# FNet mixing plus an MLP on one core: layer norm of blocks 2 and 3 a block sooner, five staging places for the weight forms, and steps behind bank copies

## The chip, the core and the metric

The kernel runs on one core of one Trainium2 chip, as one program and one launch. The metric is the device time in microseconds (us). TensorE is written PE, VectorE DVE, ScalarE ACT, GpSimd POOL and SyncE SP, as the profile writes them. Each engine takes its instructions strictly in the order in which the program issues them, so a step that waits holds everything behind it on the same engine; SP's and ACT's DMA issues stand in those orders too.

## The reference

```python
x = A_x                                   # (1, 2048, 640), float32
xn = layernorm(x, axis=-1)                # eps 1e-5
a = einsum("bsd,ed->bse", xn, dft_hid_re) # hidden DFT, 640 x 640
b = einsum("bsd,ed->bse", xn, dft_hid_im)
y = einsum("ts,bse->bte", dft_seq_re, a) - einsum("ts,bse->bte", dft_seq_im, b)  # 2048 x 2048
h = gelu_tanh(einsum("bsd,df->bsf", xn, w1) + b1)    # 640 -> 1536
out = x + y + (einsum("bsf,fd->bsd", h, w2) + b2)    # 1536 -> 640
```

## The kernel before

**Numbers.** Every product is made of three matmuls: each operand is split into a high and a low part (`split`, lines 160 and 161: ACT copies the high part, DVE subtracts it to get the low part), and high x high, high x low and low x high are added up in a PSUM bank (`product`, lines 277 to 279). A matmul has a 128x128 weight and 512 columns.

**Tokens** are handled in four blocks t = 0 to 3 of 512, that is 16 chunks c of 128 rows; block t has chunks 4t to 4t+3. For one chunk the layer norm is `load_x` (SP), `ln_stats` (DVE), `ln_scale` for four chunks at once (with a square root on ACT), `ln_apply` (DVE, then four stores by SP into the scratch tensor `xs`, line 203). `load_z` (line 234) reads a whole block back from `xs` in another layout, and `transpose_z`, `turn_z2`, `turn_z1` turn it on DVE.

**Stage 1, the MLP of blocks 0 and 1.** The loop over g has 12 steps i for each block; a step is `hidden` (15 matmuls), `gelu` (ACT line 314 and 318, DVE line 320) and `output` (15 matmuls), with the GELU two steps ahead of `output`. Beside block 0's steps runs `first_block(i)`, beside block 1's `second_block(i)`. These hold the layer norm of later blocks, the splits of weights, and from `w_early` the first six steps of `prep_w`.

**`prep_w(s)`** makes the forms of the hidden DFT matrices that the end of the kernel reads back: for column group j = s // 3 it turns two raw pieces (`turn_w`, DVE), and `put_w` splits them by parts into a staging place and stores each into `wits` (line 400). Of the three sub-steps k = s % 3 the first puts two forms, the second two, the third three. During block 1 the staging place is one of two tiles `wst`; later it is one of two halves of the tile `HS`. The store is issued by ACT. A new put into a place waits for the store that last read it.

**Stage 2, the hidden layer of blocks 2 and 3** together, in six passes q, each over two of the twelve units, by a scheme of sums and differences with fewer products. Its inputs (`form_of`: a11, a12, a22, s1 to s4, oa, ob) are made from blocks 2 and 3 (`load_z(2)`, `load_z(3)`) at the end of block 1; its weight sums by `load_rq`, `sums_w1`, `split_w1`. A pass is `head(q)` (12 matmuls), `mid(q)` (21) and `finish(q)` (21). `head` and `mid` hold `copy_bank` (ACT, line 801), which copies a half-finished sum to another bank before PE adds more to the first. `mid` calls `between`, and `outs(1)` (the call `rest`) runs inside `mid(0)`. `act` is the GELU of a pass (line 845). The steps 6 to 14 of `prep_w` run beside passes 1 to 4 (`late_steps`).

**Stage 3, the second layer of blocks 2 and 3**: 24 steps n of 15 matmuls (`second`), with `beside_second(n)`: `split_h` makes the moving operand of two later steps, `late_w2` splits w2, `formed` and `build` make the forms of the rows for stage 4 from pairs of rows `xr` (`load_xr`, line 565) and store the first four, `outs(2)` adds the biased result of block 2 to its x (`load_xo(2)`, line 339) on POOL (line 349), and `load_a` loads the first pieces of the sequence matrices.

**Stage 4** is the sequence DFT and the hidden DFT up to the end, from some 418 us on.

A tile of a pool, or a `place(tag)`, that is opened where another was, waits for all readers and writers of the earlier one. The places `xc01`, `as` and `r01` are used several times in this way; `zo` is one tile shared in turn by z, xo and wz.

Of the kernel before, what the change touches and what calls it, by code (L numbers as in the profile page):

```python
# [26 lines left out]
def kernel(  # L27
# [152 lines left out]
    def ln_stats(c):  # L180
        m = MV
        st = ST[c % 2]
        half = D // 2
        for h in range(2):
            nc.vector.bn_stats(st[:, h, :], xt[c][:, h * half : (h + 1) * half])
        nc.vector.bn_aggr(m[:, c % 4, 0:2], st.rearrange("p a b -> p (a b)"))
# [198 lines left out]
    def put_w(w, j, main, odd=None, negative=False):  # L385

        n = GWIDE[w] * P
        if A["w"]:
            t = A["w"].tile([P, 2, 3 * P], F32R, tag="wst", bufs=2, name=f"wst{w}_{j}")
        else:  # L390
            A["nst"] = A.get("nst", 0) + 1
            t = HS[:, 1 + A["nst"] % 2, :, : 3 * P]
        split(t[:, 0, : 2 * P], t[:, 1, : 2 * P], main)
        if odd is not None and not negative:
            split(t[:, 0, 2 * P :], t[:, 1, 2 * P :], odd)
        elif odd is not None:
            h, l = t[:, 0, 2 * P :], t[:, 1, 2 * P :]
            nc.scalar.activation(h, odd, AF.Copy, scale=-1.0)
            nc.vector.scalar_tensor_tensor(l, odd, -1.0, h.bitcast(F32), op0=ALU.mult, op1=ALU.subtract)
        stores.append(lambda: nc.scalar.dma_start(wits[w][j], t[:, :, :n].bitcast(F32)))  # L400
        if len(stores) == 2:
            put_away()

# [148 lines left out]
    def load_xr(k):  # L552
        if k >= len(builds):
            return
        h, c = builds[k]
        xr[k] = []
        if k == len(builds) - 1:
            A["xcp", 2] = place("xc23", (P, 2, 2, 7 * P))
        for half in range(2):
            if k == len(builds) - 1:  # L560

                r = A["xcp", 2][:, 1, half, :D].bitcast(F32)
            else:
                r = row_tile(f"xr{k}_{half}")
            nc.sync.dma_start(r, xs[half * NS // 2 + h * NK + c])
            xr[k].append(r)
# [171 lines left out]
    def two(lo):  # L738
        return A["zs"][:, lo * TB : (lo + 2) * TB].rearrange("p (a b) -> p a b", a=2)
# [137 lines left out]
    def first_block(i):  # L877

        if i < 2:
            ln_apply(2 * i)  # L880
            ln_apply(2 * i + 1)
            load_x(4 + 2 * i)
            load_x(5 + 2 * i)
        if 2 <= i < 6:
            ln_stats(4 + i - 2)
        if i == 6:
            ln_scale(4, 4)
            for c in range(4, 8):
                ln_apply(c)
            load_z(1)  # L890
            for c in range(8, 12):
                load_x(c)
        if i in (8, 9):
            transpose_z(1, i - 8)
        if 8 <= i < 12:
            ln_stats(i)

    def open_w():
        es_e.close()
# [19 lines left out]
    def second_block(i):  # L919

        if i == 0:
            open_w()
            ln_scale(8, 4)
            for c in range(8, 12):
                ln_apply(c)
            for c in range(12, 16):
                load_x(c)
        if i == 1:
            load_z(2)
        if 2 <= i < 6:  # L930
            ln_stats(10 + i)
        if i == 3:
            A["zs"] = place("xc01", (P, 30 * P), F32, name="zs")
            turn_z2(two(0), 0)
            turn_z2(two(2), 2)
        if i == 4:
            turn_z1(ZT[:, 0], 4)
            form_of("a11", 0, two(0)[:, 0], lane("as", 5))
        if i == 6:
            ln_scale(12, 4)  # L940
            for c in range(12, 16):
                ln_apply(c)
            load_z(3)
            form_of("a11", 1, two(0)[:, 1], lane("xc23", 0))
            form_of("oa", 0, ZT[:, 0], lane("xc23", 1))
            form_of("a12", 0, two(2)[:, 0], lane("xc23", 2))
        if i == 7:
            open_tw()
            open_xf()
        if i == 8:  # L950
            turn_z2(ZT, 2)
            turn_z2(two(4), 0)
            turn_z1(A["zs"][:, 6 * TB : 7 * TB], 4)
            sums_w1(0)
        if i == 9:
            load_xo(1)
            split_w1(0)
            load_rq(1)
            form_of("a22", 0, ZT[:, 0], lane("r01", 0))
            form_of("a22", 1, ZT[:, 1], lane("r01", 1))  # L960
            add(ZT, ZT, two(4))
            form_of("s1", 0, ZT[:, 0], lane("r01", 2))
            form_of("s1", 1, ZT[:, 1], lane("r01", 3))
# [13 lines left out]
        form_of("s4", 0, two(2)[:, 0], XTT[:, 3])  # L977
        form_of("s4", 1, two(2)[:, 1], XTT[:, 4])

    w_early = {1: (0,), 2: (1,), 3: (2,), 4: (3,), 5: (4, 5)}  # L980
    gelu(0, acc0)
    gelu(1, acc1)
    for g in range(NG):
        t, i = divmod(g, NF)
        if t == 0:
# [2 lines left out]
            load_w1(i + 6)  # L988
            load_w2(i + 4)
            first_block(i)  # L990
            if i == 10:
                load_xo(0)
            if i == NF - 1:
                acc = hidden(g + 2)
                output(g)
# [77 lines left out]
    head(1)  # L1073
    finish(0)
    open_wz()
    late_steps = {1: (6, 7), 2: (8, 9), 3: (10, 11), 4: (12, 13, 14)}
    for q in range(1, NF // 2):
        p = q - 1
        if not p % 2:
            act(p, 0, 0)  # L1080
        sums_w1(q + 1)
        act(p, 0, 1)

        def between():
            split_w1(q + 1)
            act(p, 1, 0)
            act(p, 1, 1)

        mid(q, between)
        for k in late_steps.get(q, ()):  # L1090
            prep_w(k)
        load_rq(q + 2)
        if q < NF // 2 - 1:
            head(q + 1)
        else:
            split_h(0)
            second(2, 0, 0, HU[0, 0])
            split_h(1)
            for u in (2, 3, 4):
                split_w2(u)  # L1100
                raw_w2(u + 4, u - 2)
        finish(q)
        if q == 4:
            for u in range(2, 6):
                raw_w2(u, u - 2)

# [8 lines left out]
    A["asb"] = place("as", (P, 48 * P), name="asb")  # L1115
    A["sums"] = A["asb"][:, 20 * P : 38 * P].bitcast(F32).rearrange("p (a b) -> p a b", a=2)

    def formed(k):
        build(k)
        nc.sync.dma_start(forms_ab[k], A["xab", k].bitcast(F32))  # L1120
        nc.sync.dma_start(forms_c[k], A["xc", k].bitcast(F32))

    def late_w2(u):
        split_w2(u)
        if u + 4 < 11:
            raw_w2(u + 4, (u + 2) % 4)

    def beside_second(n):

        if n % 2 and 2 <= (n + 3) // 2 < NF:  # L1130
            split_h((n + 3) // 2)
        if 1 <= n <= 6:
            late_w2(n + 4)
        if n in (2, 4, 6, 8):
            formed(n // 2 - 1)
            load_xr((2, 3, 4, 6)[n // 2 - 1])
# [1 line left out]
            load_xo(2)  # L1138
        if n == 9:
            build(4, "ab")  # L1140
        if n == 10:
            build(6, "ab")
        if n == 11:
            outs(2, (3, 4, 0, 1, 2))
            A["es"].close()
            A["raw"] = pool("rawp")
            load_a(0)
            load_a(1)
        if n == 14:
            A["xcp", 0] = place("xc01", (P, 2, 2, 7 * P))  # L1150
            build(4, "c")
            load_xr(5)
        if n == 16:
            build(5)
        if n == 17:
# [550 lines left out]
```

## Time and profile before

| | |
|---|---|
| time, median of 2 runs | 938.42 us (937.73 to 939.11) |
| profiled execution, own time | 940.44 us |
| its span, first to last instruction | 938.7 us |
| mean granted clock of PE | 0.966 of full speed |
| busy share of the span | PE 92%, DVE 70%, ACT 38%, POOL 2% |
| matmuls | 3711 |
| moved by DMA | 158.43 MB, 169 GB/s in the mean |

How to read it: a busy PE says little about when matmuls are late, so the prediction counts matmuls by stretches of time. In a row of a table of stretches stand the stretch, its length, the busy time of each engine with the number of its instructions in brackets, the granted clock of PE, the busy share of the DMA engines and GB/s. In a timeline row stand the start, the duration, the engine (SPq and ACTq are the issuing of DMAs), the line, the operation, the tiles, the count, and in square brackets the idle time before it with what ended it. In a list of waits stand who waited at which line for whom, the sum in us, the number of times and the longest.

### The profile page before, as it was taken

To read this page: it belongs to the slowest core of one execution; us is meant where nothing else is said; L and a number is where in the kernel's file an instruction comes from. 1 tells how busy PE (TensorE), PEld (TensorE's weight loads), DVE (VectorE), ACT (ScalarE), POOL (GpSimd) and SP (SyncE) were. 2 spreads that over 40 slices of the span, in tenths; PEclk is the share of its full clock that TensorE was granted. 3 is DMA by queue.
4 is the path that set the end of the run, shared out by engine and by line. 5 is a ranking of instruction groups with operands and counts; after the bars stand their busy time and mean duration, and the time that the engine had idled before them with its cause. 6 is when DMAs were issued, how large, how long until landed. Compare 5 with 4: busy or idle time off the path is not lost.

```text
span 938.7 us, 10279 instructions
## 1 busy us (share of the span) xinstructions
PE 866.1 (92%) x3711; PEld 707.4 (75%) x3711; DVE 660.8 (70%) x831; ACT 354.4 (38%) x495; POOL 22.0 (2%) x22
## 2 busy tenths in 40 slices
PE   8999998749765997899999999999999999999997
PEld 6888886537554786677888888888888888888886
DVE  7556535376433395469798888889896889887587
ACT  6444422434332554144334334433232332323241
POOL 0000200003000001100000000000000000000000
PEclk9999999978987899989999999999999999999999
DMA  6746584545553497859487535985475588934355
GB/s 186 221 134 172 113 239 135 128 99 117 155 160 118 138 356 220 202 109 190 103 198 161 148 78 151 319 228 114 130 192 158 181 257 206 291 116 163 97 154 113
DMA packets 214913, 158.43 MB, mean 169 GB/s; under 512 B 82896, under 2 KB 189648, under 8 KB 214352
## 3 DMA queue, kind: packets, MB, share of 16 engines
q1 hardware_dynamic: 201088, 145.08, 59.0%
q10 hardware_dynamic: 13776, 12.72, 3.9%
q8 instruction: 29, 0.48, 0.2%
q14 instruction: 20, 0.16, 0.1%
HBM read 114.76 MB, written 42.99 MB: 168 GB/s over the span
## 4 chain that ended last, share of the span: by engine, by line
PE 58%; DMA 8%; DVE 4%; ACT 2%; SPq 2%; issue 1%; POOL 1%; POOLq 0%; ACTq 0%; DVEq 0%
PE banks L278 19%; PE banks L277 19%; PE banks L279 19%; DMA wit<-hs 3%; DMA forms_c<-xcst 2%; DMA xo<-in_A_x_dram 1%; DMA xr<-xs 1%; SPq L477 1%; DVE hs L161 1%; POOL xo L349 1%; DMA rq<-in_B_w_dram 1%; DVE asb L437 0%; DVE rq L437 0%; ACT xcst L589 0%; DVE rt L497 0%
## 5 line engine op out<-in xcount | busy, mean ns | idle before, releaser
L278 PE MATMUL banks<-as,xab 128*128 128x512 f32 x411 | 160.2, 390 | 0.8 <-DVE as L161 0.8
L279 PE MATMUL banks<-as,xab 128*128 128x512 f32 x411 | 160.2, 390 | 0.0
L277 PE MATMUL banks<-as,xab 128*128 128x512 f32 x411 | 160.1, 390 | 0.0
L160 ACT ACTIVATE as<-r 128x1024 fp32r<-128x1024 f32 x80 | 85.0, 1062 | 175.0 <-PE banks L279 148.5
L161 DVE TENSOR_TENSOR as<-r,as 128x1024 fp32r<-128x1024 f32 x80 | 97.2, 1216 | 38.5 <-ACT as L160 38.4
L278 PEld LDWEIGHTS banks<-as,xab 128*128 128x128 f32 x411 | 77.3, 188 | 17.4 <-DVE as L161 1.2
L279 PEld LDWEIGHTS banks<-as,xab 128*128 128x128 f32 x411 | 77.3, 188 | 16.1
L277 PEld LDWEIGHTS banks<-as,xab 128*128 128x128 f32 x411 | 77.3, 188 | 16.0
L277 PE MATMUL banks<-as,xc 128*128 128x512 f32 x224 | 87.1, 389 | 0.0
L278 PE MATMUL banks<-as,xc 128*128 128x512 f32 x224 | 87.1, 389 | 0.0
L279 PE MATMUL banks<-as,xc 128*128 128x512 f32 x224 | 87.1, 389 | 0.0
L160 ACT ACTIVATE as<-rt 128x1024 fp32r<-128x1024 f32 x32 | 34.0, 1062 | 69.9 <-PE banks L279 57.9
L301 PE MATMUL banks<-xtt,xab 128*128 128x512 f32 x240 | 56.7, 390 | 0.0
L301 PEld LDWEIGHTS banks<-xtt,xab 128*128 128x128 f32 x240 | 44.9, 188 | 9.5 <-DVE xtt L161 0.2
L278 PEld LDWEIGHTS banks<-as,xc 128*128 128x128 f32 x224 | 42.0, 188 | 8.8
L279 PEld LDWEIGHTS banks<-as,xc 128*128 128x128 f32 x224 | 42.0, 188 | 8.8
L277 PEld LDWEIGHTS banks<-as,xc 128*128 128x128 f32 x224 | 42.0, 188 | 8.7
L320 DVE TENSOR_TENSOR hs<-ab,hs 128x512 fp32r<-128x512 f32 x24 | 17.6, 735 | 40.2 <-ACT hs L318 40.1
L161 DVE TENSOR_TENSOR as<-rt,as 128x1024 fp32r<-128x1024 f32 x32 | 38.8, 1212 | 5.3 <-ACT as L160 5.3
L497 DVE STREAM_TRANSPOSE r<-raw 128x1024 f32<-128x1024 f32 x32 | 39.5, 1240 | 1.5 <-PE banks L279 1.0
L160 ACT ACTIVATE as<-u 128x1024 fp32r<-128x1024 f32 (+1 forms) x24 | 22.1, 919 | 48.2 <-PE banks L279 48.2
L437 DVE TENSOR_TENSOR r<-r,rt 128x1024 f32<-128x1024 f32 x32 | 38.9, 1219 | 0.1
(328 smaller groups left out, 1625.7 us busy)
## 6 DMA issues: line engine op xcount, KB each, us to landing
raw<-in_A_dft_seq_re_dram SPq DMA_DIRECT2D x64, 256.0 KB, 5.2
raw<-in_A_dft_seq_im_dram SPq DMA_DIRECT2D x64, 256.0 KB, 5.3
ws<-wit SPq DMA_DIRECT2D x15, 384.0 KB, 5.7
x<-in_A_x_dram SPq DMA_DIRECT2D x16, 320.0 KB, 4.4
xs<-x SPq DMA_DIRECT2D x64, 80.0 KB, 1.8
xo<-in_A_x_dram SPq DMA_DIRECT2D x16, 320.0 KB, 6.7
xab<-wit SPq DMA_DIRECT2D x13, 384.0 KB, 4.0
wit<-hs ACTq DMA_DIRECT2D x12, 384.0 KB, 3.8
```

The source lines that it names most:

```text
L160: nc.scalar.activation(h, s, AF.Copy)
L161: nc.vector.tensor_tensor(l, s, h.bitcast(F32), op=ALU.subtract)
L277: nc.tensor.matmul(acc, wh, mh, start=first, stop=False, skip_group_check=goes_on)
L278: nc.tensor.matmul(acc, wh, ml, start=False, stop=False, skip_group_check=goes_on)
L279: nc.tensor.matmul(acc, wl, mh, start=False, stop=last, skip_group_check=goes_on)
L301: nc.tensor.matmul(acc, W1[i][:, a, j * P : (j + 1) * P], XT[j][:, b], start=n == 0, stop=n == len(steps) - 1)
L320: nc.vector.tensor_tensor(hs[:, 1], a, hs[:, 0].bitcast(F32), op=ALU.subtract)
L349: eng.tensor_tensor(d, d, yt.rearrange("p (n i) -> p n i", i=B), op=ALU.add)
L437: nc.vector.tensor_tensor(dst, a, b, op=op)
L477: nc.sync.dma_start(raw[g][q * B : (q + 1) * B], v[:, :, s0 : s0 + NK * B])
L497: nc.vector.transpose(held(pieces[g][2], u).rearrange("p c (n i) -> p c n i", i=B), r.rearrange("p n (c i) -> p c n i", i=B))
```

## The change

- **Layer norm.** In `first_block` the statistics of chunks 8 to 11 move from steps 8 to 11 into steps 8 and 9; the scaling, the stores of block 2's rows and the loads of chunks 12 to 15 move from step 0 of `second_block` to step 10 of `first_block`. In `second_block`, `load_z(2)` moves from step 1 to 0, the statistics of chunks 12 to 15 from steps 2 to 5 into 0 and 1, their scaling and stores from step 6 to 2, `load_z(3)` from 6 to 3, `turn_z1` of z2 from 4 to 3, the opening of the pool `xf` with `load_rq(0)` from 7 to 5, the turns of z3 with `sums_w1(0)` from 8 to 7, `load_xo(1)` from 9 to 7, `split_w1(0)` and `load_rq(1)` from 9 to 8. Step 5 of `prep_w` moves from step 5 to step 6.
- **Staging.** From step 6 of `prep_w` on, a put goes to one of five places in a new tile at `xc01` instead of two in `HS`, and SP issues the store instead of ACT.
- **Order in a pass.** `prep_w` comes behind `head(q + 1)` instead of ahead of it; `load_rq(q + 2)` moves into `between`; step 14 moves behind `finish(4)`; the split of w2 unit 4 moves from pass 5 to step 1 of stage 3.
- **Stage 3.** The rows of build 5 are loaded at the start, into a free part of the place `as`, instead of at step 14; the first two parts of build 6 move from step 10 to 12, behind `outs(2)`; `load_a(1)` moves from 11 to 13.

```diff
--- before.py
+++ after.py
@@ -388,8 +388,8 @@
         if A["w"]:
             t = A["w"].tile([P, 2, 3 * P], F32R, tag="wst", bufs=2, name=f"wst{w}_{j}")
         else:
-            A["nst"] = A.get("nst", 0) + 1
-            t = HS[:, 1 + A["nst"] % 2, :, : 3 * P]
+            A["nst"] = A.get("nst", -1) + 1
+            t = A["wst"][:, A["nst"] % 5 * 6 * P :][:, : 6 * P].rearrange("p (a b) -> p a b", a=2)
         split(t[:, 0, : 2 * P], t[:, 1, : 2 * P], main)
         if odd is not None and not negative:
             split(t[:, 0, 2 * P :], t[:, 1, 2 * P :], odd)
@@ -397,7 +397,7 @@
             h, l = t[:, 0, 2 * P :], t[:, 1, 2 * P :]
             nc.scalar.activation(h, odd, AF.Copy, scale=-1.0)
             nc.vector.scalar_tensor_tensor(l, odd, -1.0, h.bitcast(F32), op0=ALU.mult, op1=ALU.subtract)
-        stores.append(lambda: nc.scalar.dma_start(wits[w][j], t[:, :, :n].bitcast(F32)))
+        stores.append(lambda: (nc.scalar if A["w"] else nc.sync).dma_start(wits[w][j], t[:, :, :n].bitcast(F32)))
         if len(stores) == 2:
             put_away()
 
@@ -560,6 +560,8 @@
             if k == len(builds) - 1:
 
                 r = A["xcp", 2][:, 1, half, :D].bitcast(F32)
+            elif k == 5:
+                r = A["asb"][:, (38 + 5 * half) * P : (43 + 5 * half) * P].bitcast(F32)
             else:
                 r = row_tile(f"xr{k}_{half}")
             nc.sync.dma_start(r, xs[half * NS // 2 + h * NK + c])
@@ -892,8 +894,15 @@
                 load_x(c)
         if i in (8, 9):
             transpose_z(1, i - 8)
-        if 8 <= i < 12:
-            ln_stats(i)
+            ln_stats(2 * i - 8)
+            ln_stats(2 * i - 7)
+        if i == 10:
+            load_xo(0)
+            ln_scale(8, 4)
+            for c in range(8, 12):
+                ln_apply(c)
+            for c in range(12, 16):
+                load_x(c)
 
     def open_w():
         es_e.close()
@@ -920,42 +929,41 @@
 
         if i == 0:
             open_w()
-            ln_scale(8, 4)
-            for c in range(8, 12):
+            load_z(2)
+            ln_stats(12)
+            ln_stats(13)
+        if i == 1:
+            ln_stats(14)
+            ln_stats(15)
+        if i == 2:
+            ln_scale(12, 4)
+            for c in range(12, 16):
                 ln_apply(c)
-            for c in range(12, 16):
-                load_x(c)
-        if i == 1:
-            load_z(2)
-        if 2 <= i < 6:
-            ln_stats(10 + i)
         if i == 3:
             A["zs"] = place("xc01", (P, 30 * P), F32, name="zs")
             turn_z2(two(0), 0)
             turn_z2(two(2), 2)
+            turn_z1(ZT[:, 0], 4)
+            load_z(3)
         if i == 4:
-            turn_z1(ZT[:, 0], 4)
             form_of("a11", 0, two(0)[:, 0], lane("as", 5))
+        if i == 5:
+            open_xf()
         if i == 6:
-            ln_scale(12, 4)
-            for c in range(12, 16):
-                ln_apply(c)
-            load_z(3)
             form_of("a11", 1, two(0)[:, 1], lane("xc23", 0))
             form_of("oa", 0, ZT[:, 0], lane("xc23", 1))
             form_of("a12", 0, two(2)[:, 0], lane("xc23", 2))
         if i == 7:
             open_tw()
-            open_xf()
-        if i == 8:
             turn_z2(ZT, 2)
             turn_z2(two(4), 0)
             turn_z1(A["zs"][:, 6 * TB : 7 * TB], 4)
+            load_xo(1)
             sums_w1(0)
-        if i == 9:
-            load_xo(1)
+        if i == 8:
             split_w1(0)
             load_rq(1)
+        if i == 9:
             form_of("a22", 0, ZT[:, 0], lane("r01", 0))
             form_of("a22", 1, ZT[:, 1], lane("r01", 1))
             add(ZT, ZT, two(4))
@@ -977,7 +985,7 @@
         form_of("s4", 0, two(2)[:, 0], XTT[:, 3])
         form_of("s4", 1, two(2)[:, 1], XTT[:, 4])
 
-    w_early = {1: (0,), 2: (1,), 3: (2,), 4: (3,), 5: (4, 5)}
+    w_early = {1: (0,), 2: (1,), 3: (2,), 4: (3,), 5: (4,), 6: (5,)}
     gelu(0, acc0)
     gelu(1, acc1)
     for g in range(NG):
@@ -988,8 +996,6 @@
             load_w1(i + 6)
             load_w2(i + 4)
             first_block(i)
-            if i == 10:
-                load_xo(0)
             if i == NF - 1:
                 acc = hidden(g + 2)
                 output(g)
@@ -1073,7 +1079,8 @@
     head(1)
     finish(0)
     open_wz()
-    late_steps = {1: (6, 7), 2: (8, 9), 3: (10, 11), 4: (12, 13, 14)}
+    A["wst"] = place("xc01", (P, 30 * P), name="wstp")
+    late_steps = {1: (6, 7), 2: (8, 9), 3: (10, 11), 4: (12, 13)}
     for q in range(1, NF // 2):
         p = q - 1
         if not p % 2:
@@ -1083,24 +1090,25 @@
 
         def between():
             split_w1(q + 1)
+            load_rq(q + 2)
             act(p, 1, 0)
             act(p, 1, 1)
 
         mid(q, between)
-        for k in late_steps.get(q, ()):
-            prep_w(k)
-        load_rq(q + 2)
         if q < NF // 2 - 1:
             head(q + 1)
         else:
             split_h(0)
             second(2, 0, 0, HU[0, 0])
             split_h(1)
-            for u in (2, 3, 4):
+            for u in (2, 3):
                 split_w2(u)
                 raw_w2(u + 4, u - 2)
+        for k in late_steps.get(q, ()):
+            prep_w(k)
         finish(q)
         if q == 4:
+            prep_w(14)
             for u in range(2, 6):
                 raw_w2(u, u - 2)
 
@@ -1115,6 +1123,8 @@
     A["asb"] = place("as", (P, 48 * P), name="asb")
     A["sums"] = A["asb"][:, 20 * P : 38 * P].bitcast(F32).rearrange("p (a b) -> p a b", a=2)
 
+    load_xr(5)
+
     def formed(k):
         build(k)
         nc.sync.dma_start(forms_ab[k], A["xab", k].bitcast(F32))
@@ -1122,15 +1132,15 @@
 
     def late_w2(u):
         split_w2(u)
-        if u + 4 < 11:
+        if u + 4 < NF - 1:
             raw_w2(u + 4, (u + 2) % 4)
 
     def beside_second(n):
 
         if n % 2 and 2 <= (n + 3) // 2 < NF:
             split_h((n + 3) // 2)
-        if 1 <= n <= 6:
-            late_w2(n + 4)
+        for u in {1: (4, 5), 2: (6,), 3: (7,), 4: (8,), 5: (9,), 6: (10,)}.get(n, ()):
+            late_w2(u)
         if n in (2, 4, 6, 8):
             formed(n // 2 - 1)
             load_xr((2, 3, 4, 6)[n // 2 - 1])
@@ -1138,18 +1148,18 @@
             load_xo(2)
         if n == 9:
             build(4, "ab")
-        if n == 10:
-            build(6, "ab")
         if n == 11:
             outs(2, (3, 4, 0, 1, 2))
             A["es"].close()
             A["raw"] = pool("rawp")
             load_a(0)
+        if n == 12:
+            build(6, "ab")
+        if n == 13:
             load_a(1)
         if n == 14:
             A["xcp", 0] = place("xc01", (P, 2, 2, 7 * P))
             build(4, "c")
-            load_xr(5)
         if n == 16:
             build(5)
         if n == 17:
```

## The prediction

> **What bounds the kernel now.** PE is busy for 92% of the span, so I looked for the stretches in which its matmuls are not back to back. The table of stretches, cut where its gaps begin and end:
>
> ```profile
> 145.00:186.00 41.00, 32.34 (x130) 24.82 (x128) 18.43 (x44) 16.91 (x31) 0.00 (x0) 0.96 0.42 123
> 186.00:205.00 19.00, 5.96 (x19) 4.52 (x20) 13.50 (x17) 5.58 (x10) 0.00 (x0) 0.64 0.71 142
> 205.00:222.00 17.00, 12.88 (x43) 9.72 (x42) 12.91 (x19) 8.54 (x15) 7.27 (x5) 0.80 0.38 92
> 222.00:312.00 90.00, 65.50 (x249) 50.94 (x248) 36.62 (x79) 33.90 (x71) 0.00 (x0) 0.87 0.48 136
> 312.00:364.00 52.00, 50.59 (x222) 41.33 (x221) 35.26 (x66) 26.77 (x48) 0.00 (x0) 1.00 0.80 285
> 364.00:374.00 10.00, 4.84 (x16) 3.54 (x16) 5.97 (x10) 6.43 (x11) 3.15 (x3) 0.83 0.54 100
> 394.00:418.00 24.00, 18.01 (x66) 13.97 (x65) 18.71 (x29) 9.85 (x16) 0.00 (x0) 0.79 0.40 92
> 440.00:915.00 475.00, 475.00 (x2098) 393.21 (x2097) 398.41 (x364) 165.94 (x169) 0.00 (x0) 1.00 0.64 173
> ```
>
> The last row sets the scale: 475 us for 2098 matmuls is 0.2264 us each, clock 1.00. Nothing is to be won there, and what is won earlier passes whole to the end. Length less matmuls x 0.2264 is what each other stretch loses, slow clock included: 11.6, 14.7, 7.3, 33.6, 1.7, 6.4 and 9.1 us, together 84.4. The list of PE's waits names the causes:
>
> ```profile
> PE banks L277 <- ACT banks L801: 24.0, 5, 10.4
> PE banks L277 <- ACT r L160: 14.6, 1, 14.6
> PE banks L277 <- ACT hs L318: 6.5, 2, 4.1
> PE banks L277 <- ACT xtt L160: 5.5, 1, 5.5
> PE banks L277 <- DVE ot L347: 5.2, 1, 5.2
> PE banks L277 <- ACT pb L845: 4.4, 2, 3.2
> ```
>
> These waits make 60.2 us; most of the other 24 is slow clock and half-fed restarts after them. So the question is, for each wait, what made ACT or DVE late, and whether the change takes that away.
>
> **Block 1 (145 to 205, 26.3 lost).**
>
> ```profile
> 92.30 0.88 DVE L185 BATCH_NORM_STATS2 st<-x 128x6 f32<-128x320 f32 x2
> 119.47 0.69 ACT L314 ACTIVATE ab<-banks,b1c 128x512 f32<-128x512 f32 x1 [0.87 <-DVE wt L437]
> 131.57 7.80 SPq L364 DMA_DIRECT2D wraw<-in_A_dft_hid_re_dram  x4
> 165.69 0.69 ACT L314 ACTIVATE ab<-banks,b1c 128x512 f32<-128x512 f32 x1 [1.06 <-DVE wst L161]
> 169.51 2.18 DVE L201 TENSOR_SCALAR x<-x,mv 128x640 f32<-128x640 f32 x4
> 170.15 8.93 SPq L203 DMA_DIRECT2D xs<-x  x16
> 180.66 1.91 SPq L234 DMA_DIRECT2D z<-xs  x4
> 189.00 1.25 DVE L730 STREAM_TRANSPOSE zt<-z 128x1024 f32<-128x1024 f32 x1 [14.15 <-DMA z<-xs]
> 199.02 1.29 DVE L161 TENSOR_TENSOR r<-zt,r 128x512 fp32r<-128x512 f32 x2 [0.69 <-ACT r L160]
> ACT wst L160 <- DMA wit<-wst: 16.8, 7, 5.4
> ```
>
> The GELU of step 6 starts at 165.69, the scaling that follows it ends at 171.7, 16 stores take SP until 179.1, block 3 is read from 180.66 and is there at 189.00, and the form for which PE waits 14.6 us (s1) is done 11.3 us later, at 200.3. After the change the scaling follows step 2, whose GELU starts at 119.47: with the same 6.0 us the rows are ready at 125.5. On SP stand ahead of their stores the loads of the next wraw pieces, after step 1's turn at about 118, at worst twice 7.80 us: 134. Stores to 143, z3 issued then and landed 8.3 us after: 152 at worst, s1 possible at 163. PE, without the 14.6 and without the some 10 us lost before, asks for it at 199.0 - 24.6, about 174. So this wait goes with 11 us in hand.
>
> What is late next is ACT itself. Line 318's 6.5 us come from puts that wait for their stores; in block 1 the places stay two and ACT still issues, so much of the 16.8 us of store waits stays. What lightens it: step 5 moves to a step of its own, and DVE no longer meets rows that have not landed. The GELU runs two steps ahead, two times 30 matmuls, 13.6 us; that cover bore the first lag before. I keep 3 us of loss, with 0 and 10 (all that was lost before the z wait) as ends.
>
> The moved parts in block 0: two more chunks of statistics (0.88 and an aggregate each, some 2.2 us) stand ahead of block 1's operand on DVE in step 9. PE waits for nothing there now; the cover is 30 matmuls of `output`, 6.8 us, so 0; uncovered it would be 2.2. Square roots and their table loads keep their number. SP's 16 stores and four loads move ahead of `outs(0)`'s stores, and wraw and z2 stand behind both; all are awaited steps later. `load_z(2)` has to wait for the landed stores of block 0's output (one tile `zo`), as before. Gain 26.3 - 3 = 23.3.
>
> **The first `copy_bank` (205 to 222, 7.3 lost).**
>
> ```profile
> 204.24 0.58 ACT L808 ACTIVATE fifth<-banks 128x512 f32<-128x512 f32 x1
> 212.45 0.58 ACT L801 ACTIVATE banks<-banks 128x512 f32<-128x512 f32 x1 [1.51 <-DVE ab L347]
> ```
>
> From `fifth` to the end of this copy ACT and DVE need 8.8 us in one chain (forms of s3, weight sums, ob, bias and transposition of one bank), which the change leaves alone. But `fifth` was late, behind forms waiting for z3. Now it can follow its matmuls, and PE has 30 more (6.8 us) before it needs the copy: 2.0 stay, 5.3 go. Ends: 0 and 7.3.
>
> **The passes (222 to 312, 33.6 lost).** Groups of instructions in this stretch, the store's own issue, and the last put before the longest wait:
>
> ```profile
> L161 DVE TENSOR_TENSOR hs<-wz,hs 128x256 fp32r<-128x256 f32 (+1 forms) x30 | 10.5, 378 | 21.9 <-ACT hs L160 21.9
> L160 ACT ACTIVATE hs<-wz 128x256 fp32r<-128x256 f32 (+1 forms) x30 | 10.4, 380 | 32.9 <-DMA wit<-hs 25.3 <-DVE wz L372 5.4 <-DVE wz L437 2.0
> L437 DVE TENSOR_TENSOR rq<-rq 128x256 f32<-128x256 f32 (+1 forms) x12 | 6.2, 513 | 11.9 <-DMA rq<-in_B_w_dram 11.6
> L437 DVE TENSOR_TENSOR banks<-banks,fifth 128x512 f32<-128x512 f32 x9 | 6.1, 694 | 5.1 <-ACT banks L801 4.8 <-PE banks L279 0.3
> L437 DVE TENSOR_TENSOR wz<-wz 128x256 f32<-128x256 f32 (+1 forms) x15 | 5.9, 395 | 0.2
> L161 DVE TENSOR_TENSOR tw<-rq,tw 128x1024 fp32r<-128x1024 f32 x4 | 4.9, 1226 | 11.9 <-ACT tw L160 11.9
> L372 DVE STREAM_TRANSPOSE wz<-wz 128x640 f32<-128x640 f32 x6 | 4.7, 820 | 0.0
> L400 ACTq DMA_DIRECT2D wit<-hs x21: 520/521/592, 233.1 to 304.1; - x21
> 303.23 0.42 ACT L160 ACTIVATE hs<-wz 128x256 fp32r<-128x256 f32 x1 [2.75 <-DMA wit<-hs]
> ```
>
> ACT sat 25.3 us waiting for stores to leave the two halves of HS, and `copy_bank` stood behind it. Three things go. Five places take the puts of a whole pass (4, 5, 5, 4, then 3): a place is used again a pass later, so the 25.3 go. The 21 issues (0.52 each, 10.9 us) leave ACT. And the copies now stand ahead of the steps. `load_rq` ahead of the wz loads on SP takes the 11.6 us of DVE too, which stand behind the 4.4 of line 845.
>
> What remains: ACT's puts over four passes are 10.4 busy + 5.4 + 2.0 = 17.8, 4.5 a pass, and stand between `fifth` and the next copy, where PE has 36 matmuls, 8.2 us. DVE's six rows make 38.3, 9.6 a pass, against 54 matmuls, 12.2 us. So neither binds in the mean; passes 1 and 4, with two turns and the three dependent sums, do more than their quarter, and step 14 adds three puts ahead of the last copy. I keep 1.5 us a pass, 6, with 0 and 16 as ends.
>
> New waits: SP's stores stand ahead of later loads on SP, each until DVE has its low part; behind them wait the w2 loads of units 2 to 5, needed only after pass 5 and a step of stage 3 (21 + 15 + 21 + 15 matmuls, 16 us). The split of w2 unit 2 now waits until the last staging store has left `xc01`, with the same cover. Gain 27.6.
>
> [...]
>
> **Stage 3 (364 to 374 and 394 to 418).**
>
> ```profile
> 361.78 8.83 DMA xo<-in_A_x_dram
> 364.74 0.52 ACT L589 ACTIVATE xab<-xr 128x384 fp32r<-128x384 f32 x1 [5.53 <-DMA xr<-xs]
> 370.85 5.03 POOL xo L349 x4
> 386.83 8.19 DMA xr<-xs
> 395.10 0.52 ACT L589 ACTIVATE xab<-xr 128x384 fp32r<-128x384 f32 x1 [14.10 <-DMA xr<-xs]
> ```
>
> The second place first: PE waits for a `split_h` that stands on ACT behind build 5, which waits 14.1 us for its rows, because they were issued at 386.83. They are now loaded some 60 us sooner, into free columns of `as`; SP waits there for the last weights in `as` (end of pass 5), and behind it stand only loads that wait for stage 3 anyway. 9.1 lost, 0.5 stays: gain 8.6.
>
> The first place I expect to move, not to go. Build 6 (5.53 us for rows) no longer holds up `outs(2)`, so PE gets its two banks in time. But POOL's first add still waits for xo, landed at 370.6 by the chain, and two buffers let DVE turn only two banks before that. The other three come after POOL's adds, 1.26 us each, so at about 375.4; then build 6 and the `split_h` that PE needs after 12 + 30 matmuls, 9.5 us behind 364.5: wanted at 374.0, there at about 379. That is as long a gap as the 5.2 now. Gain 0; ends -1 and 6.4.
>
> **How the numbers follow.** 23.3 + 5.3 + 27.6 + 8.6 = 64.8 us from the profiled execution's own 940.44 gives 875.6; the median shown is 2.0 lower than that execution, so **874**, chance 0.57, own range 864 to 885.
>
> Rivals. **Block 1 stays held** (0.12): ACT's store waits in two places let the GELU come late, all 10 stay instead of 3, and the first copy keeps its 7.3: 886. For it: 16.8 us of waits untouched; against: the x rows no longer stop DVE. **The passes become hand-over bound** (0.10): ACT and DVE take turns 30 times, DVE's idle 21.9 in its row stays in part, 16 us stay instead of 6: 884; with the former together 896. Against: of that idle most is the stores'. **Only the issues leave ACT** (0.04): stores land so much later from SP's fuller queue that places are still waited for, and 10.9 of the 33.6 us go instead of 27.6: 890. Against: the row at 303.23 waited for a place used two puts before; now it is five. **xo does not matter** (0.08): if the first place goes too, 867. **The order stands on paper only** (0.05): wraw, stores and z3 queue on SP so that s1 comes after 174; it would have to be 11 us later than my worst case, and then up to 14.7 return: 888. **Slower than before** (0.04): the clock. If the denser matmuls made the granted clock fall through the 475 us and after, the gain of 65 would be used up where it falls under 0.88 (2098 x 0.2264 / 0.88 = 540). Against: 475 us at 1.00 in this trace. [...]
>
> The range, with the two mishaps together on one side and all ends good on the other: 858 to 898. Two runs of this kernel differ by 0.15%, but about 2% is what a measurement can tell from no change: faster than 919.7 has 0.92, within 2% 0.05, slower 0.03.
>
> **What would show it.** Right: z's landing some 40 us sooner and no wait for line 160's r; no put waiting for a store after 222 and line 801's wait under 4 us in all; no wait of build 5 for xr; a gap near the middle of block 3's second layer, ended by a `split_h` behind DVE's transpositions, with POOL waiting for xo. Wrong: long waits for line 318 still in block 1, a turn of wz waiting for its loads in pass 1, or SP's stores holding back rq.

## The result and the profile after

The changed kernel takes **876.99 us** (876.81 to 877.18) against 938.42 before: ratio 0.9345, 95% interval 0.9305 to 0.9386. Its profiled execution has a span of 875.0 us and an own time of 876.81.

First the table of engines on its page, then the table of stretches, cut again where the gaps begin and end (stretch, length, busy time of each engine with its instructions, granted clock, DMA share, GB/s):

```profile
PE 849.2 (97%) x3711; PEld 698.5 (80%) x3711; DVE 659.7 (75%) x831; ACT 354.0 (40%) x495; POOL 21.2 (2%) x22
```

```profile
145.00:181.00 36.00, 33.45 (x144) 26.50 (x143) 23.60 (x42) 15.63 (x31) 0.00 (x0) 1.00 0.72 189
181.00:200.00 19.00, 13.41 (x47) 10.08 (x46) 14.48 (x22) 9.92 (x18) 7.26 (x5) 0.82 0.38 90
200.00:254.00 54.00, 54.00 (x240) 44.72 (x239) 34.93 (x77) 30.95 (x66) 0.00 (x0) 1.00 0.66 186
254.00:316.00 62.00, 60.20 (x263) 49.02 (x263) 38.41 (x71) 34.76 (x62) 0.99 (x1) 1.00 0.88 300
316.00:331.00 15.00, 9.83 (x32) 7.35 (x32) 13.03 (x24) 5.44 (x10) 5.41 (x5) 0.77 0.74 153
331.00:376.00 45.00, 44.18 (x196) 36.24 (x195) 34.04 (x43) 18.92 (x26) 0.00 (x0) 1.00 0.87 168
376.00:851.00 475.00, 475.00 (x2097) 393.47 (x2096) 398.45 (x364) 165.98 (x169) 0.00 (x0) 1.00 0.64 173
```

The last stretch, the sequence DFT, is what it was: 475 us, 2097 matmuls, clock 1.00. All that changed lies ahead of it, and PE's busy time (849.2) is now 97% of the span. Length less matmuls x 0.2264, against what the prediction left standing:

| part | lost before | forecast to stay | stays |
|---|---|---|---|
| block 1 (145 to 181) | 26.3 | 3 | 3.4 |
| first `copy_bank` (181 to 200) | 7.3 | 2.0 | **8.4** |
| passes (200 to 254), and their hand-over to stage 3 (254 to 316) | 33.6 | 6 | 0 and 2.5 |
| stage 3, first place (316 to 331) | 6.4 | 6.4 | 7.8 |
| stage 3, second place (331 to 376) | 9.1 | 0.5 | 0.6 |

Together 22 to 23 us stay where the prediction left 19.6 (with 1.7 between the passes and the first place). PE's list of waits (who waited where for whom: us, times, longest) has changed as much:

```profile
PE banks L277 <- ACT banks L803: 5.0, 1, 5.0
PE banks L277 <- ACT xtt L160: 3.3, 1, 3.3
...
PE banks L278 <- DVE xtt L161: 1.9, 1, 1.9
...
PE banks L277 <- ACT r L160: 0.8, 1, 0.8
```

Line 803 is `copy_bank` (801 before): 24.0 us in five waits have become one of 5.0. The 14.6 for line 160's r (the form of s1) is down to 0.8. The 3.3 and 1.9 are the `split_h` of stage 3's first place.

### The profile page after: what moved, and what is told of

Same layout as the page of the kernel before. It is cut to its first block, busy times and chain, and to the rows that moved or that the text cites. A ratio compares the mean times of both kernels' runs of the same rounds, so it can differ in the third digit from the quotient of the medians.

```text
span 875.0 us, 10292 instructions
## 1 busy us (share of the span) xinstructions
PE 849.2 (97%) x3711; PEld 698.5 (80%) x3711; DVE 659.7 (75%) x831; ACT 354.0 (40%) x495; POOL 21.2 (2%) x22
## 4 chain that ended last, share of the span: by engine, by line
PE 74%; DMA 7%; DVE 7%; ACT 4%; SPq 3%; issue 2%; POOL 1%; ACTq 0%; DVEq 0%; POOLq 0%
PE banks L278 23%; PE banks L279 23%; PE banks L277 23%; PE banks L301 4%; DMA forms_c<-xcst 2%; DMA wit<-wst 2%; POOL xo L349 1%; DMA x<-in_A_x_dram 1%; DMA xo<-in_A_x_dram 1%; DMA xs<-x 1%; SPq L876 1%; SPq L364 1%; DMA wraw<-in_A_dft_hid_im_dram 1%; SPq L203 1%; DVE xtt L161 0%
## 5 line engine op out<-in xcount | busy, mean ns | idle before, releaser
L161 DVE TENSOR_TENSOR as<-u,as 128x1024 fp32r<-128x1024 f32 (+1 forms) x24 | 24.9, 1042 | 18.8 <-ACT as L160 18.8
```

The lines of the kernel that those rows point to most:

```text
L161: nc.vector.tensor_tensor(l, s, h.bitcast(F32), op=ALU.subtract)
```

## Experiments: one part undone at a time

Each kernel below is the changed one with one part put back. Times stand beside 876.99.

**u_ln: the layer norm and `second_block` as before.**

```diff
-        if i == 10:
-            load_xo(0)
-            ln_scale(8, 4)
...
+        if i == 6:
+            ln_scale(12, 4)
+            for c in range(12, 16):
+                ln_apply(c)
+            load_z(3)
```

> The changed kernel with the layer norm of blocks 2 and 3 and the steps of second_block put back where they were before. If the parts add up, the losses of block 1 (26.3 us before, 3.7 now) come back and the first copy stays near 8: about 22 us more, 899. If the passes ran well only because block 3's data came early, the copies of the passes wait again and it goes over 910. If the layer norm is not the cause of the gain in block 1, it stays under 885.

Measured 900.06 us, ratio 0.9598 (0.9574 to 0.9623): 23.1 more. The wait list of that run:

```profile
PE banks L277 <- ACT r L160: 14.3, 1, 14.3
PE banks L277 <- ACT hs L318: 6.2, 2, 4.1
```

The old waits of block 1 (14.6 and 6.5) are back to within 0.3 us, and the passes still lose nothing. The sooner layer norm, with the steps of `second_block` that moved along with it, therefore pays for block 1 by itself; the two were not run apart.

**u_stage, u_two, u_act: the staging.** The first has two halves of HS and ACT's stores again (the new order stays), the second two halves with SP's stores, the third five places with ACT's stores.

```diff
# u_stage and u_two
-            t = A["wst"][:, A["nst"] % 5 * 6 * P :][:, : 6 * P].rearrange("p (a b) -> p a b", a=2)
+            t = HS[:, 1 + A["nst"] % 2, :, : 3 * P]
# u_stage and u_act
-        stores.append(lambda: (nc.scalar if A["w"] else nc.sync).dma_start(wits[w][j], t[:, :, :n].bitcast(F32)))
+        stores.append(lambda: nc.scalar.dma_start(wits[w][j], t[:, :, :n].bitcast(F32)))
```

> The changed kernel with the old staging (two halves of HS, stores issued by ACT) and the new order in a pass. My theory, that places are the larger part: puts wait some 25 us for stores again, 6.3 us a pass beside the 4.5 of the puts, against 8.2 us of cover, so 2 to 3 us a pass come back: about 10 more, 887. Rival, that the order alone does it, because the copies stand ahead: within 3 us of 877. Rival, that the places alone do it: the whole 33 us come back, 910.

> The changed kernel with SP issuing the stores, but two halves of HS as places. My theory: the waits for stores come back in full, some 20 to 25 us of ACT, and most of the 20 us with them: 890 to 897. Rival, that the issuer counts: under 882.

> The changed kernel with five places, but the stores issued by ACT again. My theory, that the places carry the 20 us which the old staging cost: only 21 issues of some 0.5 us and their waits for DVE's low parts come back to ACT, about 4 us a pass beside 4.5 of puts, within or just over the cover of 8.2: 877 to 881. Rival, that ACT must not issue: half of the 20 us or more come back, 887 or over.

| | two places | five places |
|---|---|---|
| ACT issues | 896.62 (ratio 0.9555, 0.9532 to 0.9578) | 885.17 (0.9436, 0.9415 to 0.9457) |
| SP issues | 893.56 (0.9519, 0.9505 to 0.9533) | 876.99 |

ACT's waits for stores and the stretch of the passes in u_stage, then the same waits in u_two; in the third fence u_act's waits of ACT between 225 and 275 us, and its stores by line:

```profile
ACT hs L160 <- DMA wit<-hs: 19.9, 11, 2.7
...
217.00:284.00 67.00, 52.30 (x192) 39.93 (x191) 32.26 (x64) 29.30 (x58) 0.00 (x0) 0.85 0.52 159
```

```profile
ACT hs L160 <- DMA wit<-hs: 20.2, 9, 5.2
```

```profile
ACT wstp L160 <- DVE wstp L161: 2.6, 2, 1.3
ACT pa L847 <- DVE wstp L161: 2.1, 2, 1.1
L400 ACTq DMA_DIRECT2D wit<-wstp x21: 326/327/632, 211.1 to 258.8; - x21
```

Two places make ACT wait 20 us for stores whoever issues them, so the places are the larger part: 16.6 us with SP as issuer, 11.5 with ACT. The issuer is worth 3.1 us while the places still block (the two intervals touch), and 8.2 once they do not. I had expected at most 4 of it; the u_act expectation is a miss. So is u_stage's: 887 was expected, or 910 if the places did it all, and 896.62 came, 19.6 more. u_two's was right. The last row is the line of the stores: 21 issues of 0.33 to 0.63 us, added up one by one 8.9 us. That alone could make the 8.2. The two rows above it point at a second cost: an issue on ACT comes after DVE's low part, and the next put or GELU (line 847) stands behind it. How the 8.2 divide between the two was not separated.

**u_order: `prep_w` ahead of `head(q + 1)` again**, five places and SP kept.

```diff
         mid(q, between)
+        for k in late_steps.get(q, ()):
+            prep_w(k)
```

> The changed kernel with five places and SP's stores, but with the steps of prep_w ahead of head(q + 1) again. My theory: without store waits a pass's puts are some 4.5 us of ACT, and PE has 27 matmuls (6.1 us) between the copy's source and its use, so 0 to 6 us come back in all: 877 to 883. Rival, that the order is what counts: the copies are late by the puts each pass and 15 to 20 us come back, 892 to 897.

Measured 876.21 us, 0.9342 (0.9321 to 0.9363), the same. With five places the order of the steps is worth nothing: no put waits any more, so it does not matter whether the copy stands behind it. With two places it may well matter (33.6 us lost in the passes before, 23.5 in u_stage, 67.00 - 192 x 0.2264), but the order alone with two places was not run.

**u_xr5: the rows of build 5 at step 14 again.**

```diff
-    load_xr(5)
...
             build(4, "c")
+            load_xr(5)
```

> The changed kernel with the rows of build 5 loaded at step 14 again. My theory: build 5 waits for rows behind SP's loads of the sequence matrices and holds up a split_h: a gap near 345 us of some 9 us, 886. Rival, that the gap near 318 already pays for it, because PE comes later there: under 3 us more, 880.

Measured 886.40 us, 0.9448 (0.9422 to 0.9474): 9.4 more, and ACT's timeline has the old wait back:

```profile
339.18 0.53 ACT L589 ACTIVATE xab<-xr 128x384 fp32r<-128x384 f32 x1 [10.68 <-DMA xr<-xs]
```

## Experiments: what still stands

**e_xo2: `load_xo(2)` at step 7 of stage 3 instead of 8.** In the changed kernel, timelines of SP, POOL, DVE and ACT at the first place:

```profile
301.46 1.85 SPq L567 DMA_DIRECT2D xr<-xs  x2
303.36 2.97 SPq L339 DMA_DIRECT2D xo<-in_A_x_dram  x4
315.01 6.40 POOL L349 TENSOR_TENSOR xo<-xo,ot 128x512 f32<-128x512 f32 x5 [117.20 <-DMA xo<-in_A_x_dram]
316.34 0.72 DVE L347 STREAM_TRANSPOSE ot<-banks 128x512 f32<-128x512 f32 x1 [9.66 <-POOL xo L349]
320.32 0.42 ACT L591 ACTIVATE xab<-asb 128x256 fp32r<-128x256 f32 x1 [10.10 <-DVE asb L437]
322.89 1.21 DVE L161 TENSOR_TENSOR xtt<-pb,xtt 128x1024 fp32r<-128x1024 f32 x1
```

xo is issued at 303.36, behind the stores and row loads of step 8, and is there at 315.01. DVE's third transposition waits 9.66 us for POOL; build 6 (line 591) waits 10.10 behind it; the low part of the `split_h` that PE needs is done at 324.1.

```diff
+        if n == 7:
+            load_xo(2)
...
-        if n == 8:
-            load_xo(2)
```

> The changed kernel with the load of x for block 2 (load_xo(2)) at step 7 of stage 3, ahead of the forms and rows of step 8 on SP, instead of behind them. My theory, that xo's late landing holds DVE's transpositions and behind them build 6 and split_h(8): xo lands some 8 us sooner and the gap near 318 (3.4 + 2.2 us and slow clock, 8.0 in all) goes to 0 to 2, 869 to 871. Rival, that POOL's adds or build 6 set it: the gap stays over 4 us, 874 or more.

Measured **868.94 us** (868.87 to 870.88), ratio 0.9264 (0.925 to 0.9278), and the place as a stretch of its trace, with SP's and POOL's rows:

```profile
316.00:331.00 15.00, 15.00 (x68) 12.43 (x67) 13.09 (x28) 8.36 (x14) 0.00 (x0) 1.00 1.16 230
...
296.18 2.96 SPq L339 DMA_DIRECT2D xo<-in_A_x_dram  x4
...
308.46 6.28 POOL L349 TENSOR_TENSOR xo<-xo,ot 128x512 f32<-128x512 f32 x5 [110.63 <-DMA xo<-in_A_x_dram]
```

PE is busy for all 15 us where it was busy for 9.83. Loading xo 7 us sooner (296.18 against 303.36) removed the whole gap, so its late landing was the cause. This version beats both kernels.

**e_outs0 and e_chain: the first `copy_bank`.** ACT in the changed kernel, from the forms of s2 to the copy:

```profile
180.05 0.63 ACT L160 ACTIVATE xfx<-zt 128x512 fp32r<-128x512 f32 x1 [3.16 <-issue]
181.62 0.58 ACT L810 ACTIVATE fifth<-banks 128x512 f32<-128x512 f32 x1
186.20 1.06 ACT L160 ACTIVATE tw<-rq 128x1024 fp32r<-128x1024 f32 x1 [2.44 <-DVE rq L437]
187.68 0.64 ACT L344 ACTIVATE banks<-banks,b2c 128x512 f32<-128x512 f32 x1
189.84 0.58 ACT L803 ACTIVATE banks<-banks 128x512 f32<-128x512 f32 x1 [1.51 <-DVE ab L347]
```

e_outs0 puts the eviction of `outs(1, (0,))` (line 344) ahead of the weight sums. e_chain, built on e_xo2, puts `sums_w1(1)`, `split_w1(1)`, `load_rq(2)` and the form ob behind the copy, at the head of `rest`.

```diff
# e_outs0
+    outs(1, (0,), yt=lambda n: AB[:, 0], done=False)
     sums_w1(1)
...
# e_chain
     def rest():
+        sums_w1(1)
+        split_w1(1)
+        load_rq(2)
+        form_of("ob", 0, A["zs"][:, 6 * TB : 7 * TB], HS[:, 0])
         outs(1, (2, 1, 3, 4), yt=lambda n: AB[:, (n + 1) % 2])
```

> The changed kernel with outs(1, (0,)), which frees the bank for the first copy, ahead of the sums and the split of the next weights and of ob. My theory, that the first copy is late because these 3.5 us of ACT and DVE stand ahead of it: the gap of 5.2 us near 185 falls under 2 and its slow clock goes, 5 to 8 us less, 869 to 872. Rival, that the forms of s2 and s3, which come late from block 3, set it: 1 us or less, 876.

> Built on the kernel that loads xo of t = 2 at n = 7 (868.94 us). `sums_w1(1)`, `split_w1(1)`, the load of rq and the form ob go behind the first `copy_bank`, so that only the eviction of `outs(1, (0,))` stands ahead of it. Theory A (the copy stands behind that work on ScalarE): the eviction runs at about 183.9, its transposition at 184.6, the copy ends near 186 in place of 190.4 and the wait of 5.0 us ends under 1.5; but the banks of `head(1)` then wait for `outs(1, (2, ...))`, which gives back 2 to 4 of the 6 us: 864 to 867 us. Rival B (VectorE is busy without a break from 177 to 199 and only the place of the stall changes): 868 to 870 us.

e_outs0 takes 877.16 us, 0.9348 (0.9331 to 0.9366). e_chain takes 868.83, 0.9263 (0.925 to 0.9275), beside e_xo2's 868.94. Neither gains, as both rivals said. In e_outs0 the copy itself still stands on ACT behind the split of the weights and starts at 188.79 instead of 189.84, so e_chain is the real test. PE's waits, e_outs0 first, then e_chain:

```profile
PE banks L277 <- ACT banks L803: 4.4, 1, 4.4
```

```profile
PE banks L277 <- DVE ab L347: 3.7, 1, 3.7
...
PE banks L277 <- ACT banks L803: 0.5, 1, 0.5
```

In e_chain the copy is no longer late (0.5 us), but PE then waits 3.7 us for the next bank to be turned by DVE; the place loses 8.2 us in place of 8.6 (both counted from the starts of the matmuls). The stall moved behind the next thing that DVE had to do. So the place of the copy on ACT alone is not what costs; the forms, sums and transpositions from some 177 to 199 us are DVE's and ACT's work, and it starts late.

**e_turn, best2 and e_z3: starting it sooner**, all built on e_xo2. DVE stands idle for 5.60 us ahead of 162.66 in the changed kernel. e_turn moves z3's three transpositions there from step 7 (ahead of `prep_w(5)`), and a22 and s1 from step 9 to 8; best2 is e_turn with e_chain; e_z3 is e_turn with the scaling and stores of rows 12 to 15 at step 1.

```diff
# e_turn, best2, e_z3: in step 6
             form_of("a12", 0, two(2)[:, 0], lane("xc23", 2))
+            turn_z2(ZT, 2)
+            turn_z2(two(4), 0)
+            turn_z1(A["zs"][:, 6 * TB : 7 * TB], 4)
# e_z3 also
             ln_stats(15)
-        if i == 2:
             ln_scale(12, 4)
```

> Built on the kernel that loads xo of t = 2 at n = 7 (868.94 us). The three transpositions of z3 stand at the end of step 6 of block 1 in place of step 7, and the forms a22 and s1 follow at the end of step 8 in place of step 9. Theory A: the loss of 8.6 us around the first `copy_bank` is what VectorE has left to do late: it stands idle for 5.60 us ahead of 162.66 and is then busy from 165 to 185 almost without a break, so that `fifth` and the copy come behind the forms of s2. With the transpositions (3.1 us) in that idle stretch the forms of s2 end some 3 us sooner, the copy too, and 8.6 becomes 5 to 6: 865 to 867 us. Rival B: ScalarE's wait for the stores of the staged forms (6.17 us to 162.22) and the order of the steps on ScalarE hold the forms where they are: 868 to 870 us.

> Both of these edits on the kernel that loads xo of t = 2 at n = 7 (868.94 us). If both theories A hold, the work of VectorE that ends at 199 ends 3 us sooner and the copy no longer waits for it: 8.6 us lost become 2 to 4, 862 to 865 us. If both rivals hold: 868 to 870 us.

> The kernel with the transpositions of z3 at the end of step 6 (877.77 us, 10.0 us lost in one place of block 1), and `ln_scale` and `ln_apply` of rows 12 to 15 at step 1 of block 1 in place of step 2, ahead of `prep_w(0)` and its loads. Theory A (z3 lands too late: its stores stand behind the loads and stores of the forms of wr and wi, so that it is loaded at 156 and lands at 164): the stores go out near 118 to 128, z3 is loaded near 138, right behind the last transposition of z2, the transpositions wait for nothing, the 10 us of block 1 go, and the forms of s1 and s2 end sooner, so that the first copy loses 3 to 6 us in place of 8.6: 862 to 867 us. Rival B (the copy is late by VectorE's and ScalarE's own work from 165 on, z3 or not): the 10 us go, the first copy stays at 8 to 9: 868 to 870 us. Rival C (z3's load does not come sooner, the place of the stores alone moves): 876 to 879 us.

e_turn and best2 fell outside both theories; e_z3 has the time of its rival C, though not by C's mechanism. e_turn takes 877.77 us (0.9352, 0.9339 to 0.9364), best2 877.81 (0.9353, 0.934 to 0.9366) and e_z3 877.33 (0.9352, 0.934 to 0.9365), some 9 us over e_xo2. DVE and ACT in e_turn, and PE's wait:

```profile
164.28 1.25 DVE L732 STREAM_TRANSPOSE zt<-z 128x1024 f32<-128x1024 f32 x1 [8.09 <-DMA z<-xs]
167.58 1.20 ACTq L400 DMA_DIRECT2D wit<-wst  x2
172.06 0.42 ACT L160 ACTIVATE wst<-wt 128x256 fp32r<-128x256 f32 x1 [16.23 <-DMA wit<-wst]
PE banks L277 <- ACT hs L318: 9.9, 1, 9.9
```

z3 is not there before 164.28. The idle stretch was no room to use: the transposition in it waits 8.09 us, DVE's low parts of step 5 wait behind it, so their stores leave at 167.58 instead of 156.67; the third put needs one of the two places, waits 16.23 us on ACT, and the GELU behind it stops PE for 9.9. In e_z3, SP and ACT:

```profile
123.98 18.79 SPq L203 DMA_DIRECT2D xs<-x  x16
143.78 1.98 SPq L364 DMA_DIRECT2D wraw<-in_A_dft_hid_re_dram  x4
148.05 2.47 SPq L234 DMA_DIRECT2D z<-xs  x4
173.27 0.42 ACT L160 ACTIVATE wst<-wt 128x256 fp32r<-128x256 f32 x1 [9.21 <-DMA wit<-wst]
```

z3 is loaded 8 us sooner (148.05, against 156.00), and DVE no longer waits for it. But the 16 stores take SP 18.8 us, the loads of the next weight pieces go out at 143.78 instead of 123.76, and step 5's third put still holds ACT until 173.27. Its GELU stops PE for 6.6 us, and the clock granted in 145 to 181 is 0.91, where the changed kernel has 1.00. So block 1 in the changed kernel is in balance by little: z3's loads, the weight pieces on SP and the two staging places hold each other, and each move sooner made another late. The first copy came no sooner either: it starts at 197.29 in e_turn and at 198.50 in e_z3, against 189.84 in the changed kernel, because everything behind that put came later. Whether block 1 with more staging places would let the first copy go was not run.

## Why the prediction was right, and where its steps were off

874 was forecast, 877 came; the sum against the profiled executions was 64.8 us, and 940.44 - 876.81 = 63.6 were measured. Of the miss 1.2 us are the sum's; the rest is the step from the profiled execution to the median, put at -2.0, where the two agree after the change (876.81 and 876.99). That the sum came so close is in part luck: the first copy kept 6.4 us more than forecast, the passes with their hand-over 5.2 less (2.5 for 6 and 1.7). The low end of the range is not quite its sum: with all four good ends another 17.4 us go from 874, which gives about 857, not 858.

**Block 1: right in size, wrong in its working.** The gain is as forecast (3.4 us stay), and u_ln shows that the layer norm makes it. But z3 was forecast to land by 152 at worst, with 11 us in hand. SP in the changed kernel, with its waits for those stores between 130 and 175 us, then ACT and DVE:

```profile
132.99 2.07 SPq L364 DMA_DIRECT2D wraw<-in_A_dft_hid_im_dram  x4
140.94 13.50 SPq L203 DMA_DIRECT2D xs<-x  x16
156.00 2.12 SPq L234 DMA_DIRECT2D z<-xs  x4
SPq L203 <- DMA wit<-wst: 12.2, 3, 5.8
162.22 0.42 ACT L160 ACTIVATE wst<-wt 128x256 fp32r<-128x256 f32 x1 [6.17 <-DMA wit<-wst]
165.08 0.69 DVE L320 TENSOR_TENSOR hs<-ab,hs 128x512 fp32r<-128x512 f32 x1 [1.99 <-ACT hs L318]
165.69 1.24 DVE L732 STREAM_TRANSPOSE zt<-z 128x1024 f32<-128x1024 f32 x1
176.40 1.29 DVE L161 TENSOR_TENSOR r<-zt,r 128x512 fp32r<-128x512 f32 x2 [0.70 <-ACT r L160]
```

The weight loads were out at 135 (forecast: 134 at worst). Then, by the profile, the stores of x waited 12.2 us for the stores that ACT issues from `wst`, a wait that I did not count; they ended at 154.4 instead of 143, and s1 was ready at 177.7 instead of 163. The whole of the 11 us was used up, and not by z3 alone. The transposition at 165.69 has no idle time ahead of it, so z3 was there by then (in e_turn, which issues it at 155.81, it is there at 164.28). DVE came to it behind the GELU of its step, whose low part starts at 165.08, and that GELU stood on ACT behind the put that waited 6.17 us for a store. The 163 counted the transpositions from z3's landing; they stand in step 7, and DVE came to step 7 only at 165.69.

PE lost only 0.8 us there because its own demand came at about the same time, 176. That is luck: the 11 us in hand were gone. The rival "the order stands on paper only" had its condition met (s1 after 174), but not its price of up to 14.7. The sign "z's landing some 40 us sooner" failed too: the transposition starts 23 us sooner, at 165.69 against 189.00.

**First copy: the step that failed.** "Now it can follow its matmuls" was the step. The chain from `fifth` to the copy took 181.62 to 190.42, 8.8 us as forecast. But `fifth` still stands on ACT behind the forms of s2, which come at 180 to 181, while the last matmul that it needs starts at 178.19. The term of 2.0 measures 8.4 (its upper end was 7.3), and it is the largest miss; line 801's wait, now 803, is 5.0 where under 4 was the sign. An estimate from these rows: with `fifth` at 178.6 the copy would have ended near 187.4, some 2 us after PE ran out of matmuls at about 185.3, as forecast. The other 3 us of the wait of 5.0 are `fifth`'s lateness, and the slow clock after the wait (0.58 granted in 190 to 197), which the term left out, is most of what is left of the 8.4.

e_chain shows that this is no matter of the order on ACT alone. That z3's landing is the cause is not shown: in e_z3 its transpositions start at 164.33 without a wait, and the copy is later still. What ACT and DVE did late in all three kernels (the changed one, e_turn, e_z3) comes behind step 5's third put and its wait for a store, to 162.22, 172.06 and 173.27. Whether that put is the cause stays open; a version that removes the loss was not found.

**Passes: right, and over-kept.** No put waits after 200, `copy_bank`'s waits there are gone, and PE is busy for 54.00 of 54 us: of the 6 kept, 2.5 stay, and those at the hand-over to stage 3. The two-by-two table gives the staging its size, 19.6 us, and the rival that only issues leave ACT fell: five places with ACT as issuer already gain 11.5. What won the rest of the 33.6 no run separates; u_stage differs from the kernel before in the order and in `load_rq`, and in block 1 and stage 3. That rival's 10.9 was the time of the 21 issues themselves in the kernel before (0.52 us each). In the runs the issuer saved 3.1 or 8.2 us by the places beside it, and u_act's issues come to 8.9.

**Stage 3: right.** The second place went (u_xr5 brings it back with 9.4 us, forecast 8.6). The first moved and did not go, by the mechanism told: xo's landing, POOL, DVE's transpositions, build 6, `split_h`. It costs 7.8 instead of 6.4, a little past the term's end of 1 us more, and e_xo2 removes it by moving xo alone. The rival in which xo does not matter (867) is refuted as a reason, though e_xo2 ends near its number.

**Rivals on the clock and on the order.** The granted clock is 1.00 through the 475 us as before, so the denser matmuls cost nothing there. The order of `prep_w` is worth nothing beside five places; the prediction counted it among three causes of one gain, and could not have told them apart.

## What to carry to other kernels

Find for each wait of the bound engine the one resource behind it, and ask what it has to be late for next: here the number of staging places was worth 11 to 17 us, while e_chain's new order on ACT moved a stall without shortening it. An idle stretch on an engine is room only for work whose data are there (in e_turn DVE waited 8.09 us in it); look up the landing of the load, not the start of the idle time, before moving a step into it. The other way round, data that land sooner gain nothing while the step that uses them stands behind a step that waits (in the changed kernel z3's transposition behind the put that waited 6.17 us); look up both times, and take the later one. When moving a load on a shared queue, price all that is queued around it, stores of other engines' staging included (12.2 us of waits for the stores of x).

## What the runs showed of the hardware

**A stall of PE can cost more than its length, and does not always.** PE's rows in u_two, with the stretch around them (clock 0.79), and in u_ln, each after a gap:

```profile
220.32 0.50 PE L277 MATMUL banks<-xtt,tw 128*128 128x512 f32 x1 [1.87 <-ACT banks L803]
...
221.88 0.63 PE L277 MATMUL banks<-as,xab 128*128 128x512 f32 x1
222.31 0.63 PE L278 MATMUL banks<-as,xab 128*128 128x512 f32 x1
...
218.00:226.00 8.00, 6.13 (x21) 4.41 (x19) 6.21 (x13) 4.47 (x8) 0.00 (x0) 0.79 0.27 101
```

```profile
218.56 0.50 PE L277 MATMUL banks<-r,tw 128*128 128x512 f32 x1 [2.36 <-DVE banks L437]
218.90 0.40 PE L278 MATMUL banks<-r,tw 128*128 128x512 f32 x1
```

After a wait of 1.87 us the first matmuls run at full speed, and 1.6 us later they start 0.43 us apart instead of 0.23; after one of 2.36 us they don't (clock 1.00 in 208 to 274). In the kernel before, the waits of PE of 2.38, 2.73 and 3.36 us (starts at 148.10, 240.56 and 258.51) were followed by no slow matmuls either, but one of 3.19 us (268.13) was, and so were one of 3.27 us in u_act (261.14) and one of 3.41 us in e_turn (197.93). Between 60 and 420 us of the kernel before and of the changed kernel, slow matmuls followed every wait longer than 3.36 us (3.55 to 14.59). Around the first copy of the changed kernel 8.4 us are lost, 5.0 of them the wait itself. So the length of a wait alone does not tell here whether slow matmuls follow: after 1.87 us they did, after 3.36 us they did not. What decides it was not shown.

**Stores of one engine seem to hold up another engine's issues.** The profile, which infers what ends a wait, counts 12.2 us in three waits of SP for stores that ACT had issued. The stores of x read other tiles than those, so what ties them stays open.
